# Block-sparse attention with a feed-forward layer on one core: the order of ACT's squares, the type of the sums over partitions, and the step at which a sequence's first queries start

## The chip, the cores and the metric

The kernel runs on one core of one Trainium2 chip. The metric is the device time of one execution in microseconds (us), given as the median of several runs. Lower is better. The core has five engines with a queue each: TensorE (PE; its weight loads are listed apart as PEld), VectorE (DVE), ScalarE (ACT), GpSimd (POOL) and SyncE (SP), which here only issues DMAs.

## The reference

Four sequences of 768 positions go through block-sparse attention with 8 heads of 64, and the result goes through a two-layer feed-forward network with a leaky ReLU:

```python
scores = scale * np.matmul(q, k.transpose(0, 1, 3, 2))
mask = np.abs(blk_i - blk_j) <= window          # blocks of 32, window 1
mask = mask | (blk_i == 0) | (blk_j == 0) | (blk_i == n_blocks - 1) | (blk_j == n_blocks - 1)
...   # and three sampled key blocks for each query block
scores = np.where(mask, scores, -1000000000.0)
attn = np.exp(scores - max); attn = attn / (attn.sum(-1) + 1e-09)
x = (attn @ v)  as (3072, 512)
h = x @ w_in                                    # (512, 2048)
out = np.maximum(0.01 * h, h) @ w_out           # (2048, 512)
```

q, k and v are float32. The two weight matrices arrive as 64-bit floats and are 8 MB each.

## The kernel before

**Number format.** Matmuls take float16. Each operand is split into a high and a low float16 part after it is scaled by a power of two, and the products of the parts are added up in PSUM. The power of two comes from the mean square of the operand: ACT squares the tile and adds up each partition (`square`, line 230), PE adds the 128 partitions with a matmul against a 128x128 tile of ones in float32 (`scale_sum`, line 135), DVE makes the scale from the exponent with four tiny instructions (`scale_of`, lines 149 to 158), ACT writes the high part (line 594 for queries) and DVE the low part (line 596).

**Steps.** The attention is cut into 192 units, one for each pair of heads of each 64 query rows: 48 a sequence, 16 an item (256 query rows). One pass of the main loop is one step: it emits the scores of the next units (`scores`, line 714), a masked copy with the row minimum (`unit_ttr`, line 723), the exponential on ACT (`unit_exp`, line 735), the normalisation, the split in high and low part (lines 762 and 783), the DMA transposes of the split (line 788), attention times values (`pair_av`, line 815), and one chunk of the feed-forward network (`ffn_h` line 850, `ffn_act1`, `ffn_max`, `ffn_act2` lines 856 to 864, `ffn_o` line 877). A string of letters gives the order of these parts within a step. The first unit of a 64-row tile at the head of a sequence has two parts, so the first four units of a sequence have two exponentials each.

**Queries.** A load of queries covers half an item (128 rows, all heads), so there are 24, numbered n, and load n is first used at step 8n. `get_q(n)` issues the DMA (lines 528 to 532, one buffer `rq`); before that it runs the preparation of load n-1 to its end. `start_q(n)` puts the generator `prep_q` in a list, and each step's `side_step` moves every generator on by one stage. The stages of `prep_q` are: the square; nothing; the sum; the scale; the high part; the low part with the DMA transpose `qs_q<-qa_q` (line 599) and the two DMAs `qxs_q<-qs_q` that swap the halves of the partitions (lines 601 and 602). From step 11 on `get_q` is called at steps that leave 3 when divided by 8, and `start_q(n)` at step 8(n-1). Loads 6, 12 and 18 open a new sequence. `start_q(1)` is called at step 0 and again at step 2; the second call replaces the generator, and its key then stands in the list twice.

**Keys, values, weights.** Keys of the next sequence are prepared during the current one in the same manner (`prep_k`, squares at line 230), and so are the values (`prep_v`, written to a scratch tensor in DRAM as hi/lo and gathered from there). The weights are loaded, decoded (lines 363 to 367: one ACT and three DVE instructions a group), summed up in `squares` (line 201, a chain of bfloat16 matmuls) and split (lines 430 and 435) in the first 48 steps. The first two items of the feed-forward network are worked off by quarters of the weights as they come, all others once all weights are ready.

**Order.** A scheduler orders each engine's instructions at compile time by priority and by a simulated timeline: an instruction whose inputs are ready in the simulation can be put ahead of others that were emitted earlier. On the chip each engine then works through its queue in that order. `behind(begin, name)` adds an ordering edge without a semaphore, so that the new instructions stand in the queue after the named one. `square` uses it:

```python
def square(out, in_, ss):
    begin = len(nc.cur_bb.bb.instructions)
    nc.scalar.activation(out, in_, AF.Square, accum_out=ss)
    behind(begin, last_exp[0])
```

`last_exp[0]` is the newest exponential, but before the change it is set from step 48 on only (`CFG["even_at"]` is 48); until then it is `None` and the squares have no such edge.

Of the kernel before, what the change touches and what calls it, by code (L numbers as in the profile page):

```python
# [12 lines left out]
BF16 = mybir.dt.bfloat16  # L13
F32 = mybir.dt.float32
# [5 lines left out]
P = 128  # L20
# [9 lines left out]
CFG = {  # L30
    "ahead": 3,
    "av_lag": 3,
    "bs": 1500,
    "early": 2,
    "even_at": 48,
    "even": 12,
    "flag": 1,
    "g": 2,
# [34 lines left out]
def tile_block_sparse_attention_ffn(  # L73
# [19 lines left out]
    nc = tc.nc  # L93
# [17 lines left out]
    cst = ctx.enter_context(tc.tile_pool(name="cst", bufs=1))  # L111
# [12 lines left out]
    def bank(name, tag="h"):  # L124
        return ps_1.tile([P, 512], F32, tag=tag, name=name, bufs={"h": 3, "av": 1}[tag])
# [1 line left out]

    floor = cst.tile([P, 1], F32, name="floor")
    nc.vector.memset(floor, 1e-9 / PSCALE)
    ones = cst.tile([P, P], F32, name="ones")  # L130
    nc.vector.memset(ones, 1.0)

    def scale_sum(ss, n, name):
        pb = bank(f"{name}_sum")
        nc.tensor.matmul(pb[:, :n], ones, ss, start=True, stop=True)  # L135
        return pb

    def scale_of(pb, n, name, total=False, keep=None, fl="q"):
# [86 lines left out]
    last_exp = [None]  # L225
# [7 lines left out]
    def latest():  # L233
        return nc.cur_bb.bb.instructions[-1].name
# [347 lines left out]
    def prep_q(b, j, i, rq):  # L582

        nm = f"q{b}_{j}_{i}"
        ss = sm.tile([P, 1], F32, tag="ssq", name=f"ss_{nm}")
        qa = pa.tile([P, H, 2, D], F16, tag="qa", name=f"qa_{nm}", bufs=1)
        square(flat(qa)[:, :H * D], rq.rearrange("p h d -> p (h d)"), ss)
        yield 0.7
        yield 0.01
        pb = scale_sum(ss, 1, nm)  # L590
        yield 0.2
        inv, s = scale_of(pb, 1, nm)
        yield 0.4
        nc.scalar.activation(qa[:, :, 1, :], rq, AF.Copy, scale=s[:, :1])
        yield 0.7
        nc.vector.scalar_tensor_tensor(
            out=qa[:, :, 0, :], in0=rq, scalar=s[:, :1], in1=qa[:, :, 1, :], op0=ALU.mult, op1=ALU.subtract)
        qs = pa.tile([P, H, P], F16, tag="qs", name=f"qs_{nm}", bufs=2)
        nc.sync.dma_start_transpose(out=qs, in_=flat(qa))
        qxs = pa.tile([P, H, P], F16, tag="qxs", name=f"qxs_{nm}", bufs=2)  # L600
        nc.sync.dma_start(out=qxs[:D], in_=qs[D:])
        nc.sync.dma_start(out=qxs[D:], in_=qs[:D])
        last_sp["q"] = latest()
        qstack[b, j, i] = (qs, qxs, inv)
        yield 0.8
# [325 lines left out]
    def start(key, gen):  # L931
        gens[key] = gen
        flows.append(key)
# [56 lines left out]
    def refill():  # L990
        for t in list(tasks):
            if t[0] in done and t[1][0].item.nx == TPI:
                hq.extend(t[1])
                tasks.remove(t)
# [32 lines left out]
    def get_q(n):  # L1027
        if n < len(halves):
            if n >= CFG["rq"]:
                until(("q", *halves[n - CFG["rq"]]), lambda: halves[n - CFG["rq"]] in qstack)  # L1030
            rq[n] = load_q(*halves[n])

    def start_q(n):
        if n < len(halves):
            start(("q", *halves[n]), prep_q(*halves[n], rq[n]))

    def get_k(b, hp):
        n = CFG["rk"]
        ob, oh = (b, hp - n) if hp >= n else (b - 1, hp + NP - n)
        if ob >= 0 and b > 0:  # L1040
            until(("k", ob, oh), lambda: (ob, oh) in kready)
        rk[b, hp] = load_k(b, hp)

    def start_k(b, hp):
        start(("k", b, hp), prep_k(b, hp, rk[b, hp]))
# [48 lines left out]
    step = 0  # L1094
# [44 lines left out]
    for u in units:  # L1139
        it, ui = u.item, u.k * NP + u.hp  # L1140
        b, nb = it.b, it.b + 1

        if step == 2:
            start_q(1)
        if step == 6 or step % 8 == 3 and step > 8:
            get_q((step + 5) // 8 + 1)
        if step % 8 == CFG["q_at"] % 8:
            start_q(step // 8 + (2 if CFG["q_at"] < 8 else 1))
        if nb < B:
            g = it.j * 16 + ui  # L1150
            t = g - (CFG["k_at"] if b else CFG["k_at0"])
            every = CFG["k_every"] if b else 5
            if t % every == 0 and 0 <= t // every < NP:
                get_k(nb, t // every)
            if t % every == every - 2 and 0 <= t // every < NP:
                start_k(nb, t // every)
            t = g - CFG["v_at"]
            if t in (0, 2, 4, 6):
                load_v(nb, t // 2)
            if t == 8:  # L1160
                start(("v", nb), prep_v(nb))

        if u.hp == (CFG["g_at"] if step >= 4 else NP - 1) and u.T + 1 < NT:
            start_gather(b, u.T + 1)
        tc.cur_priority = max(tc.cur_priority, 1000 + step * 200)
        if step in ready:
            add_ffn(ready.pop(step))
        refill()
        backlog = len(hq) + sum(len(t[1]) for t in tasks)
        if step < CFG["even_at"]:  # L1170
            credit += max(CFG["rmin"], min(CFG["rmax"], backlog / CFG["spread"]))
            n = int(credit)
            credit -= n
        else:

            n = int(hdone[0] < len(due) and due[hdone[0]] <= step)
        if step == 0:
            scores([u])
        c = aq[0] if aq else None
        for w in CFG["ord1" if step >= CFG["ord1_at"] else "ord"]:  # L1180
            if w == "c" and c:
                ffn_act1(c)
            elif w == "m" and c:
                ffn_max(c)
            elif w == "g" and c:
                ffn_act2(c)
                oq.append(aq.popleft())
            elif w == "S" and step + 1 < len(units):
                ahead = units[step + 1:step + 3]
                if not CFG["spair"]:  # L1190
                    scores(ahead[:1])
                elif u.pi == 1:
                    if any(x.parts > 1 for x in ahead):
                        for x in ahead[:1]:
                            scores([x])
                    else:
                        scores(ahead)
                elif u.parts > 1:
                    scores(ahead[:1])
            elif w == "t":  # L1200
                while live[0] + u.parts > CFG["p"]:
                    if not pend_high and not pend_split:
                        norm_step()
                    high_step()
                    split_step()
                live[0] += u.parts
                unit_ttr(u)
            elif w == "x":
                unit_exp(u)
                if step >= CFG["even_at"]:  # L1210
                    last_exp[0] = latest()
                if u.pi == 1:
                    pend_norm.append(u.pair)
            elif w == "d":
                norm_step()
            elif w == "i":
                high_step()
            elif w == "s":
                split_step()
            elif w == "a":  # L1220
                av_step()
                if vq and vfree[0] and (vq[0][0], "ready") in scr:
                    start_gather_v()
            elif w == "v":
                ev_step()
            elif w == "b":
                do_out()
            elif w == "o":
                do_o(CFG["flag"] if hq or aq else 0)
            elif w == "p":  # L1230
                side_step(CFG["side0"] if step < 16 else CFG["side"])
                gather_step(2)
            elif w == "w":
                wcredit += [r for a, r in CFG["wr"] if step >= a][-1]
                now = tc.cur_priority
                if step < 16:
                    tc.cur_priority = now + CFG["wlate"]
                begin = len(nc.cur_bb.bb.instructions)
                while wcredit >= 1.0:
                    c = next(weights, "end")  # L1240
                    wcredit -= c if c != "end" else wcredit
                if 0 < step < 16:
                    behind(begin, last_ttr[0])
                tc.cur_priority = now
            elif w == "h":
                for i in range(n):
                    if i:
                        do_act()
                        do_o(CFG["flag"])
                    do_h()  # L1250
        step += 1
        if ui == 15:
            ready[step + CFG["lead0" if it.n == 0 else "lead1" if it.n < CFG["early"] else "lead"]] = it
# [62 lines left out]
```

## Time and profile before

| | us |
|---|---|
| median of 3 runs | 842.8 (842.22 to 843.17) |
| profiled execution, device time | 851.52 |
| profiled execution, span of the core | 849.8 |
| PE busy in the span | 749.3 (88%) |
| DVE busy | 595.5 (70%) |
| ACT busy | 507.6 (60%) |
| POOL busy | 352.8 (42%) |

The profiled execution is 8.7 us (1.0%) longer than the median of the runs. Times in the profile count from the start of its span. A row of a timeline has the start, the length, the engine, the line, the operation, out<-in, shapes and count, and in brackets the idle time of the engine ahead of it with what ended it. A row of the chain of work that ended last has the start, the length and what the end was waiting for at that time; a "q" behind an engine's name is its sequencer. A row of a table by stretches has, for each engine, the busy time and the number of instructions, then the granted PE clock as a share of the full one, the share of time in which the DMA engines were busy, and GB/s.

### The profile page before, as it was taken

Reading aid. Unit: us, or ns where it says so; the run is one execution under the profiler, and the core shown is the slowest. Engines: PE = TensorE matmul, PEld = TensorE weight load, DVE = VectorE, ACT = ScalarE, POOL = GpSimd, SP = SyncE. Lnnn points to the kernel's source line nnn. Section 1 sums busy time; section 2 is a strip of 40 time slices with the busy share of each in tenths; the row PEclk is TensorE's granted clock in tenths of the full one; section 3 lists DMA queues with packets and bytes.
Section 4 is the critical chain, followed back from the end, with each engine's and each line's share of the span. In section 5 each row is a group of like instructions: output and inputs, shape, how many; then the busy total and the mean of one; then the engine's idle time right before and its main releaser. Section 6 shows DMA issues by size and latency. Waiting matters only on the chain.

```text
span 849.8 us, 20081 instructions
## 1 busy us (share of the span) xinstructions
PE 749.3 (88%) x7140; PEld 500.6 (59%) x7140; DVE 595.5 (70%) x1595; ACT 507.6 (60%) x1199; POOL 352.8 (42%) x472
## 2 busy tenths in 40 slices
PE   1666675857798999999999999998999999999997
PEld 1455543545465666666666666665666666667664
DVE  5768889898777976867777777678666776651221
ACT  5757678776445766767566667675657556551211
POOL 0218356433233464646343455454244545332221
PEclk9977778989799999999999999999999999999999
DMA  9979289998756999996969999969586766662000
GB/s 198 273 218 247 73 176 240 245 260 147 168 131 106 175 213 190 203 179 146 197 154 154 196 182 186 202 130 204 119 155 150 125 149 139 125 129 35 26 1 25
DMA packets 312004, 135.33 MB, mean 159 GB/s; under 512 B 279774, under 2 KB 292063, under 8 KB 311903
## 3 DMA queue, kind: packets, MB, share of 16 engines
q1 hardware_dynamic: 305262, 113.59, 67.2%
q0 software_dynamic: 6640, 20.45, 9.3%
q8 instruction: 56, 0.92, 0.5%
q14 instruction: 46, 0.37, 0.2%
HBM read 65.58 MB, written 12.58 MB: 92 GB/s over the span
## 4 chain that ended last, share of the span: by engine, by line
PE 70%; DMA 12%; DVE 10%; issue 3%; ACT 2%; SPq 2%; POOL 0%; POOLq 0%; ACTq 0%; DVEq 0%
PE h L850 27%; PE o L877 26%; PE s L714 8%; PE av L815 7%; DMA pt<-pp 3%; DMA wbuf<-in_moe_w_out_dram 2%; DMA qxs_q<-qs_q 2%; DMA qs_q<-qa_q 2%; DVE p L723 2%; DVE pp L783 2%; PE turn L773 2%; DVE W L365 1%; DVE W L435 1%; DVE W L367 1%; PE q_sum L135 1%
## 5 line engine op out<-in xcount | busy, mean ns | idle before, releaser
L877 PE MATMUL o<-W,g 128*128 128x512 f16 x1152 | 270.9, 381 | 6.4 <-DVE ob L898 4.2
L850 PE MATMUL h<-x,W 128*128 128x256 f16 x2304 | 274.2, 277 | 0.2 <-DVE x L833 0.2
L850 PEld LDWEIGHTS <-W 128*128 128x128 f16 x2304 | 225.0, 100 | 37.7 <-issue 3.9
L864 POOL TENSOR_TENSOR g<-ht,g 128x512 f16<-128x512 f32 x96 | 116.9, 1217 | 304.5 <-DVE g L863 254.6
L735 ACT ACTIVATE p<-p,mx 128x384 f32<-128x384 f32 x208 | 126.2, 607 | 158.7 <-DVE mx L723 123.0
L877 PEld LDWEIGHTS <-g 128*128 128x128 f16 x1152 | 108.7, 98 | 125.6 <-issue 10.8
L656 POOL COPY kg<-kt 128x256 f16 x264 | 135.0, 540 | 45.0 <-issue 15.4
L783 DVE SCALAR_TENSOR_TENSOR pp<-p,r,pp 128x384 f16<-128x384 f32 x188 | 120.4, 666 | 24.9 <-ACT pp L762 23.6
L762 ACT ACTIVATE pp<-p,r 128x384 f16<-128x384 f32 x188 | 104.2, 604 | 23.9 <-DVE r L747 10.2
L723 DVE CUSTOM_DVE_ANT_0 p<-s,em,nsc 128x384 f32<-128x384 f32 x176 | 102.0, 608 | 19.8 <-PE s L714 17.1
L683 POOL DMA_INDIRECT vg<-scr,rows x88 | 91.3, 1037 | 50.4 <-issue 20.3
L859 DVE SCALAR_TENSOR_TENSOR ht<-ht 128x512 f32<-128x512 f32 x96 | 67.8, 706 | 53.3 <-ACT ht L856 52.7
L815 PE MATMUL av<-pt,vg 128*64 128x128 f16 x2112 | 82.1, 226 | 10.1 <-DMA pt<-pp 9.6
L815 PEld LDWEIGHTS <-vg 128*64 128x64 f16 x2112 | 73.4, 114 | 27.4 <-issue 21.7
L714 PE MATMUL s<-kg,qs_q 128*64 128x384 f16 x352 | 66.2, 351 | 25.0 <-DVE mx L723 22.7
L856 ACT ACTIVATE ht<-h,gd 128x512 f32<-128x512 f32 x80 | 53.8, 672 | 57.3 <-PE h L850 54.7
L714 PEld LDWEIGHTS <-qs_q 128*64 128x64 f16 x416 | 27.0, 111 | 79.2 <-issue 53.7
L714 PE MATMUL s<-kg,qxs_q 128*64 128x384 f16 x352 | 64.0, 343 | 5.4 <-DMA qxs_q<-qs_q 5.4
L747 DVE RECIPROCAL r<-sum 128x2 f32<-128x2 f32 x96 | 15.4, 161 | 60.2 <-ACT sum L746 57.8
L863 DVE CAST g<-ht 128x512 f16<-128x512 f32 x96 | 41.8, 435 | 9.4 <-PE o L877 7.2
L735 ACT ACTIVATION_READ_ACCUMULATOR p<-p,mx 128x1 f32 x208 | 39.0, 187 | 0.0
L714 PEld LDWEIGHTS <-qxs_q 128*64 128x64 f16 x416 | 26.2, 114 | 20.8 <-DMA qxs_q<-qs_q 9.7
(138 smaller groups left out, 758.0 us busy)
## 6 DMA issues: line engine op xcount, KB each, us to landing
vg<-scr SPq DMA_DIRECT2D x33, 256.0 KB
qxs_q<-qs_q SPq DMA_DIRECT2D x48, 128.0 KB
v<-in_v_dram SPq DMA_DIRECT2D x32, 192.0 KB
scr<-v SPq DMA_DIRECT2D x16, 384.0 KB
W<-in_moe_w_in_dram SPq DMA_DIRECT2D x5, 1024.0 KB
rq<-in_q_dram SPq DMA_DIRECT2D x20, 256.0 KB
out_dram<-ob SPq DMA_DIRECT2D x20, 256.0 KB
rk<-in_k_dram SPq DMA_DIRECT2D x24, 192.0 KB
```

Of the source, the lines that this page charges most:

```text
L656: nc.gpsimd.tensor_copy(out=kg[:, :, slot * BLOCK:(slot + 1) * BLOCK], in_=kt[:, :, bass.ds(off, BLOCK)])
L683: nc.gpsimd.indirect_dma_start(out=vg[:n_, c, :], out_offset=None, in_=scr[b][:, :], in_offset=bass.IndirectOffsetOnAxis(ap=rows[:n_, c - ...
L714: nc.tensor.matmul(o, a, k, start=(n == 0), stop=(n == 1)))
L723: nc.vector.tensor_tensor_reduce(out=u.p[i], in0=u.sp[i], in1=kgs[u.b, u.T][1] if u.T else zero.to_broadcast([P, KEYS]), scale=u.nsc, scal ...
L735: nc.scalar.activation(u.p[i], u.p[i], AF.Exp, scale=-1.0, bias=u.mx[:, :1], accum_out=u.pair.sum[:, u.pi, i:i + 1])
L762: nc.scalar.activation(pp[:, 0, :], p, AF.Copy, scale=u.r)
L783: nc.vector.scalar_tensor_tensor(out=pp[:, 1, :], in0=p, scalar=u.r, in1=pp[:, 0, :], op0=ALU.mult, op1=ALU.subtract)
L815: nc.tensor.matmul(o, a, m, start=(c == 0 and l == 0), stop=(c == n - 1 and l == 1)))
L850: nc.tensor.matmul(c.ph[:, i], w, x, start=(d == 0 and m == 0), stop=(d == NP - 1 and m == 2)))
L859: nc.vector.scalar_tensor_tensor(out=c.t, in0=c.t, scalar=0.01, in1=c.t, op0=ALU.mult, op1=ALU.max)
L864: nc.gpsimd.tensor_tensor(out=c.g[:, 1], in0=c.t, in1=c.g[:, 0], op=ALU.subtract)
L877: nc.tensor.matmul(o, a, w, start=(c.first and i == 0 and m == 0), stop=(c.last and i == 1 and m == 2)))
```

## The change

Three edits:

- `ones` becomes bfloat16, and `scale_sum` reads the upper 16 bits of each float32 partition sum as a bfloat16 (a view, no instruction is added).
- `start_q(12)` is called at step 86 instead of 88 and `start_q(18)` at step 134 instead of 136. These are the first queries of the third and the fourth sequence. All other loads, load 6 too (the test asks for a step of at least 48), keep their step. `get_q` keeps its steps.
- `last_exp[0]` is set after every exponential, so that each square emitted in the main loop before step 48 also stands behind the newest exponential in ACT's queue.

```diff
-    ones = cst.tile([P, P], F32, name="ones")
+    ones = cst.tile([P, P], BF16, name="ones")
     nc.vector.memset(ones, 1.0)
 
     def scale_sum(ss, n, name):
         pb = bank(f"{name}_sum")
-        nc.tensor.matmul(pb[:, :n], ones, ss, start=True, stop=True)
+
+        top = ss.bitcast(BF16).rearrange("p (n l) -> p n l", l=2)[:, :n, 1]
+        nc.tensor.matmul(pb[:, :n], ones, top, start=True, stop=True)
         return pb
...
-        if step % 8 == CFG["q_at"] % 8:
-            start_q(step // 8 + (2 if CFG["q_at"] < 8 else 1))
+
+        n = (step + 2) // 8 + 1
+        if step % 8 == 6 and n % 6 == 0 and step >= CFG["even_at"]:
+            start_q(n)
+        n = step // 8 + 1
+        if step % 8 == 0 and (n % 6 or step < CFG["even_at"]):
+            start_q(n)
...
                 unit_exp(u)
-                if step >= CFG["even_at"]:
-                    last_exp[0] = latest()
+                last_exp[0] = latest()
```

## The prediction

> **What bounds the kernel now.** I read the table by stretches first, because an average over the span mixes two regimes, then the chain of work that ended last, then the idle times in each engine's timeline.
>
> ```profile
> span 849.8 us, 20081 instructions
> 0.00:228.00 228.00, 143.57 (x1370) 99.36 (x1371) 189.74 (x505) 153.31 (x344) 87.32 (x120) 0.86 0.92 206
> 228.00:295.00 67.00, 62.15 (x554) 40.55 (x555) 53.12 (x157) 37.23 (x86) 24.55 (x36) 0.93 0.67 134
> 295.00:770.00 475.00, 469.68 (x4664) 311.68 (x4663) 336.13 (x904) 303.79 (x749) 224.74 (x302) 1.00 0.84 165
> ```
>
> Up to 228 us, while the weights are loaded and decoded, PE is busy 143.57 of 228 us; DVE (189.74) and the DMA engines (0.92) are the full ones there. From 295 to 770 us PE is busy 469.68 of 475 us at a granted clock of 1.00: PE is the bound. So a microsecond taken from PE's stream after about 290 us is a microsecond of the end, and one taken from ACT or DVE there is worth nothing. Before 228 us it is the other way round: what counts is when the weights are ready and PE's stream closes up.
>
> **Sums in bfloat16.** First the sums that lie in the PE-bound stretch, then what one costs on the chain.
>
> ```profile
> L135 PE MATMUL q_sum<-ss_q,ones x32: 250/260/271, 284.8 to 718.0; 128*128 128x1 f32 x32
> L135 PE MATMUL k_sum<-ss_k,ones x16: 167/250/271, 288.5 to 513.8; 128*128 128x1 f32 x16
> L135 PE MATMUL v_sum<-ssv,ones x4: 253/263/273, 389.9 to 562.7; 128*128 128x4 f32 x4
> ...
> 298.75 2.73 PE h L850 x24
> ...
> 427.22 0.31 PE q_sum L135 x2
> 427.53 2.64 PE h L850 x24
> ...
> 153.38 0.91 PE wi_sq L201 x16
> ```
>
> A float32 sum shows as two matmuls, so 32 + 16 + 4 = 52 records from 280 us on are 26 sums. A chunk of `h` takes 2.73 us on the chain without a sum ahead of it, and 0.31 + 2.64 = 2.95 us with one: a sum costs PE 0.22 us. In bfloat16 it is one matmul with a 128x128 weight load; the nearest row is line 201, bfloat16 with 128x128 weights, 0.91 us for 16, so 57 ns each. That saves 0.163 us a sum and 26 x 0.163 = 4.2 us. Bounds: 2.9 us if just one of the two passes goes (26 x 0.11), 5.7 us if the rest is free. The other 26 sums lie before 280 us, where PE has gaps; I count them at 0. The four scale instructions on DVE stay.
>
> [...]
>
> **Queries of a new sequence.** PE's idle times after 295 us are three, and two of them are the scores of a new sequence's first units that wait for `qxs_q<-qs_q`, the last DMA of `prep_q`:
>
> ```profile
> 418.24 0.49 PE L714 MATMUL s<-kt,qxs_q 128*64 128x384 f16 x3 [1.34 <-DMA qxs_q<-qs_q]
> ...
> 592.38 0.82 PE L714 MATMUL s<-kt,qxs_q 128*64 128x384 f16 x3 [2.77 <-DMA qxs_q<-qs_q]
> ...
> 621.57 1.53 PE L815 MATMUL av<-pt,v 128*64 128x128 f16 x48 [1.21 <-DMA pt<-pp]
> ...
> 592.26:595.67 3.41, 3.29 (x34) 2.67 (x35) 1.41 (x5) 1.22 (x5) 0.65 (x1) 0.50 1.03 216
> ```
>
> The second wait costs more than its 2.77 us: for the next 3.41 us the granted clock is 0.50, and half of 3.41, 1.7 us, is lost again. Together 1.34 + 2.77 + 1.7 = 5.8 us. The third wait (1.21 us) is for a transpose of the split behind load 19, which starts at step 144 in both; I leave it in.
>
> [...]
>
> Do two steps do it? Load 12, as it runs now:
>
> ```profile
> 376.01 0.69 SPq L530 DMA_DIRECT2D rq<-in_q_dram  x1
> ...
> 383.23 0.61 ACT L735 ACTIVATE p<-p,mx 128x384 f32<-128x384 f32 x1 [2.15 <-DVE mx L723]
> ...
> 400.48 0.15 DVE L149 TENSOR_SCALAR q_tot<-q_sum 128x1 f32<-128x1 f32 x1
> ...
> 403.43 0.15 DVE L158 RECIPROCAL q_s<-q_inv 128x1 f32<-128x1 f32 x1
> ...
> 408.26 0.74 DVE L596 SCALAR_TENSOR_TENSOR qa_q<-rq,q_s,qa_q 128x512 f16<-128x512 f32 x1
> ...
> 409.03 1.23 SPq L599 DMA_TRANSPOSE qs_q<-qa_q  x1
> ...
> 413.53 0.53 SPq L601 DMA_DIRECT2D qxs_q<-qs_q  x1
> ```
>
> `get_q(13)` at step 91 forces whatever is left of load 12. Started at step 88, that is the scale, the high part, the low part and the DMAs, one behind the other, from 400.48 (the first scale instruction) to 409.03 (the transpose). Started at 86, sum, scale and high part are emitted at steps 88 to 90, and only the low part and the three DMAs are left at step 91, with their input there. The low part can then go as soon as step 91 begins, about where `q_tot` stands now, and DVE has it at some 401 to 404 instead of 408.26. That is 4 to 7 us against a lateness of 1.34 and 2.77 us, so I take the whole 5.8 us; bounds 0 (the next paragraphs) and 5.8. On SP the transpose passes one `pt` transpose and a `scr<-v` store at most; `qs_q` has two buffers, and the older is free. The load is issued at 376.01 and the square would now follow the exponential of step 86 (383.23): 7 us for a load that ACT does not wait for today. Were it late, ACT would wait, but it idles 2.15 us just ahead of that exponential, and PE does not depend on it within the step.
>
> **Squares behind the newest exponential.** Before step 48 the scheduler pulled squares ahead:
>
> ```profile
> ACT qa_q L230 <- DMA rq<-in_q_dram: 12.4, 4, 6.1
> ...
> 54.16 0.63 ACT L230 ACTIVATE qa_q<-rq 128x512 f16<-128x512 f32 x1 [6.13 <-DMA rq<-in_q_dram]
> ...
> 62.70 0.60 ACT L735 ACTIVATE p<-p,mx 128x384 f32<-128x384 f32 x1
> ...
> 82.47 0.63 ACT L230 ACTIVATE qa_q<-rq 128x512 f16<-128x512 f32 x1 [4.55 <-DMA rq<-in_q_dram]
> ...
> 99.25 0.61 ACT L735 ACTIVATE p<-p,mx 128x384 f32<-128x384 f32 x1
> ...
> 55.10 0.17 DVE L747 RECIPROCAL r<-sum 128x2 f32<-128x2 f32 x1 [2.83 <-ACT sum L746]
> ...
> 84.23 0.69 DVE L364 TENSOR_SCALAR W<-W 128x1024 int32<-128x1024 int32 x1 [3.23 <-ACT W L363]
> ...
> 52.86 6.24 DMA qxs_q<-qs_q
> ...
> 74.73 13.71 DMA wbuf<-in_moe_w_out_dram
> ...
> 157.59 0.18 ACT v L230
> ```
>
> The square of load 2, emitted at step 8, stands at 54.16; the exponential of step 8 is at 62.70. ACT blocks 6.13 us on a load that has not landed, and two exponentials, a normalisation (DVE waits 2.83 us for it) and value splits queue behind. The square of load 3 (step 16, exponential at 99.25) blocks ACT for 4.55 us, and a weight decode on DVE waits 3.23 us. With the edge all four waits, 12.4 us of ACT, should go. But both large ones lie beside something longer on the chain: 52.86 to 59.1 is the DMA of load 1, 74.73 to 88.44 the load of a weight group. These end when they end, so most of the 12.4 us is hidden, and the cover is gone only if these DMAs move too. The one square that is itself on the chain is the value square at 157.59 (with its accumulate about 1 us), emitted at step 36 or later, whose exponential comes after 164; behind it, it leaves the chain. I take -1 us for this edit. Bounds: -12.4 (all of it on the path) and, from what becomes late next, the following.
>
> ```profile
> 129.59 0.72 ACT L594 ACTIVATE qa_q<-rq,q_s 128x512 f16<-128x512 f32 x1
> ...
> 135.44 0.60 ACT L735 ACTIVATE p<-p,mx 128x384 f32<-128x384 f32 x1
> ...
> 153.97 0.71 ACT L594 ACTIVATE qa_q<-rq,q_s 128x512 f16<-128x512 f32 x1
> ...
> 164.54 0.60 ACT L735 ACTIVATE p<-p,mx 128x384 f32<-128x384 f32 x1
> ...
> 165.03 1.25 SPq L599 DMA_TRANSPOSE qs_q<-qa_q  x1
> ```
>
> A later square makes a later sum, and then the high part can't be pulled ahead of the step that forces it. Load 4's high part, now at 129.59, would come near the exponential of its forcing step 27 (135.44), 5.8 us later; load 5's, now at 153.97, near that of step 35 (164.54), 10.6 us later. Load 5's transpose is issued at 165.03 today, held by SP's queue, so it loses only what passes that time. Were both delays wholly on the path, with weight loads and `pt` transposes queued behind on SP, they would cost 16.4 us.
>
> **Sum.** 4.2 + 5.8 + 1 = 11.0 us less: 838.8 for the profiled span of 849.8. The profiled execution is 1.0% longer than the median of the runs; I take the same 11.0 us off that median: 842.8 - 11.0 = 831.8.
>
> **Rivals.**
>
> *The queries stay late.* The low part and its DMAs are emitted at step 91 in both versions; if the scheduler keeps DVE's order and the transpose stays near 409, the 5.8 us stay. 842.8 - 4.2 - 1 = 837.6. For it: the forcing step does not move. Against: the scale chain between 400.48 and 408.26.
>
> *ACT's waits were on the path.* All 12.4 us come back instead of 1: 820.4. For it: DVE, the fullest engine up to 228 us, waits 2.83 and 3.23 us just because of these squares. Against: the two DMAs on the chain.
>
> *Queries of the first sequence become late (slower).* Loads 4 and 5 lose 16.4 us in full, and the start of the PE-bound stretch moves with them: 842.8 - 10.0 + 16.4 = 849.2. It decides from 11.7 us of delay on (10.0 of gain and 1.7 to be told). Against: loads 4 and 5 are first used at steps 32 and 40, five steps after the steps that force them.
>
> *No change.* The order of the first 228 us is a product of the simulated timeline; a reshuffle there that costs about the 10.0 us of the other two edits would leave 842.8.
>
> **Numbers.** Forecast (825 to 836): 0.48. Queries stay late (836 to 841): 0.19. ACT's waits on the path (818 to 825): 0.12. No change: 0.09. Slower: 0.12. A change within 0.2% (841.1 to 844.5) can't be told from none. Faster 0.79, same 0.09, slower 0.12. The range 823 to 842 holds the forecast, the late queries, and part of the two cases beside them.
>
> **What would show it.** Sums: one record a sum instead of two, line 135 below 100 ns on the chain. Queries: no idle time for `qxs_q<-qs_q` at line 714 near 410 and 585 us, no half clock there, line 599 of load 12 issued some 4 us earlier against step 91. Squares: no wait of ACT for `rq<-in_q_dram` before 130 us; the last weight decode no later than before. The prediction is wrong if PE's stream closes up later than now (about 290 us) by more than the gain, or if a new idle time takes the place of the two.

## The result, and the profile after

The change made the kernel slower: 854.47 us median (851.70 to 857.77, 5 runs) against 842.80 (841.56 to 843.86, 5 runs), ratio 1.0124 [1.0084, 1.0163]. Compared a second time, the same kernel stood at 1.0169 [1.0120, 1.0218]. The prediction was 831.8. The ratios here and below leave disturbed runs out, the medians do not, so the two can differ by 0.3%.

The profiled execution of after took 857.77 us, 3.3 us above its median; that of before was 8.7 us above its own. So the two spans (856.1 and 849.8) differ by less than the medians do, and I also use a second profile of before (e5, span 840.1).

First the head of the page of after:

```profile
span 856.1 us, 19974 instructions
PE 737.9 (86%) x7088; PEld 487.5 (57%) x7088; DVE 593.4 (69%) x1595; ACT 507.6 (59%) x1199; POOL 346.3 (40%) x472
```

and its table by stretches, cut where the weights end, where PE's stream has closed up, and 475 us on:

```profile
0.00:240.00 240.00, 143.09 (x1407) 96.55 (x1408) 190.00 (x522) 154.13 (x347) 87.69 (x122) 0.82 0.89 200
240.00:300.00 60.00, 56.06 (x497) 37.00 (x495) 48.70 (x142) 34.93 (x82) 23.37 (x35) 0.97 0.66 126
300.00:775.00 475.00, 463.60 (x4627) 304.30 (x4626) 337.35 (x903) 304.88 (x751) 219.07 (x302) 1.00 0.85 165
```

The first stretch holds the work that before did in 228 us (PE 143.09 against 143.57, DVE 190.00 against 189.74) and is 12 us longer; e5 does it in 220 us (PE 141.73, DVE 188.01). In the 475 us of the third row PE is busy 463.60 us, not 469.68 as in the 475 us from 295 us on in before: there is more idle time where PE is the bound (PE's total, 737.9 against 749.3, holds 52 records less, since each sum shows as one and not as two). The sums and the squares' edge themselves did what they should. The groups of line 137 (135 before) from 284 us on:

```profile
L137 PE MATMUL q_sum<-ss_q,ones x16: 167/177/178, 288.7 to 724.3; 128*128 128x1 bf16 x16
L137 PE MATMUL k_sum<-ss_k,ones x8: 163/172/178, 292.2 to 520.8; 128*128 128x1 bf16 x8
L137 PE MATMUL v_sum<-ssv,ones x2: 164/164/164, 397.4 to 570.5; 128*128 128x4 bf16 x2
```

A sum on the chain of work that ended last:

```profile
376.06 0.67 PE av L817 x24
376.73 0.11 PE q_sum L137
376.84 2.64 PE h L852 x24
```

ACT's waits:

```profile
ACT k_k L232 <- DMA kt<-k_k: 11.5, 4, 6.1
ACT qa_q L232 <- DMA rq<-in_q_dram: 0.5, 1, 0.5
```

PE's waits from 300 to 650 us:

```profile
PE av L817 <- DMA pt<-pp: 5.1, 2, 3.3
PE o L879 <- POOL g L866: 2.1, 3, 0.9
PE h L852 <- issue: 1.4, 1, 1.4
PE o L879 <- DVE g L865: 1.2, 1, 1.2
PE s L716 <- DVE mx L725: 0.8, 1, 0.8
PE s L716 <- DMA qxs_q<-qs_q: 0.5, 1, 0.5
```

One record a sum, and 0.11 + 2.64 = 2.75 us for a sum with its chunk, where it was 2.95. ACT waits 0.5 us for queries, where it was 12.4. PE's waits hold 0.5 us for `qxs_q`, where it was 4.1. But they hold 5.1 us for `pt` (1.2 before, 2.5 in e5), 3.3 us for g and 1.4 us of issue ahead of h (nothing of these before). And ACT now waits 11.5 us for `kt<-k_k` (6.0 before). The largest of these waits, from the timelines of ACT, DVE and SP:

```profile
206.46 0.57 ACT L858 ACTIVATE ht<-h 128x512 f32<-128x512 f32 x1
213.12 0.84 ACT L232 ACTIVATE k_k<-rk 128x768 f16<-128x768 f32 x1 [6.08 <-DMA kt<-k_k]
213.96 1.32 ACT L432 ACTIVATE W<-W,wi_s 128x512 f16<-128x512 f32 x2
...
214.70 0.75 DVE L437 SCALAR_TENSOR_TENSOR W<-W,wi_s 128x512 f16<-128x512 f32 x1 [5.54 <-ACT W L432]
...
202.04 7.43 SPq L576 DMA_TRANSPOSE kt<-k_k  x1
228.64 0.35 SPq L358 DMA_DIRECT2D wbuf<-in_moe_w_out_dram  x1
```

A key square of the next sequence stands in ACT's queue ahead of the weights' high parts. Its output buffer is free only when the transpose of the tile before has landed, and ACT blocks 6.08 us on it; DVE's low parts wait 5.54 us behind. In before that square starts at 245.65, behind the weights. The last matmul on the weights moves from 225.66 (218.08 in e5) to 237.85. PE's waits from 100 to 250 us in before, and then in after:

```profile
PE s L714 <- DVE mx L723: 17.4, 8, 4.4
PE av L815 <- DMA pt<-pp: 9.6, 2, 8.5
```

```profile
PE av L817 <- DMA pt<-pp: 31.5, 9, 8.6
PE s L716 <- DMA qxs_q<-qs_q: 9.0, 3, 4.9
PE s L716 <- DVE mx L725: 2.6, 4, 1.0
```

What PE waits for is another thing, and more of it: all rows of these two views together make 50.1 us after and 41.5 before (35.3 in e5). None of the three edits touches a `pt` transpose; the order around it is what is new. Counted in the queues, all five differ from before: the scheduler re-sorted them.

### The profile page after: what moved, and what is told of

The parts are those of the page before. It is cut to its first block, busy times and chain, and to the rows that moved or that the text cites. A ratio compares the mean times of both kernels' runs of the same rounds, so it can differ in the third digit from the quotient of the medians.

```text
span 856.1 us, 19974 instructions
## 1 busy us (share of the span) xinstructions
PE 737.9 (86%) x7088; PEld 487.5 (57%) x7088; DVE 593.4 (69%) x1595; ACT 507.6 (59%) x1199; POOL 346.3 (40%) x472
## 4 chain that ended last, share of the span: by engine, by line
PE 43%; DVE 9%; ACT 7%; DMA 4%; issue 3%; POOL 0%; SPq 0%; ACTq 0%; DVEq 0%; POOLq 0%
PE o L879 18%; PE h L852 17%; PE av L817 4%; PE s L716 4%; DVE pp L785 3%; ACT p L737 2%; DMA pt<-pp 2%; DMA kt<-k_k 2%; DVE p L725 2%; DVE ht L861 1%; ACT pp L764 1%; ACT ht L858 1%; ACT k_k L570 1%; DVE k_k L572 1%; ACT k_k L232 1%
## 5 line engine op out<-in xcount | busy, mean ns | idle before, releaser
L879 PE MATMUL o<-W,g 128*128 128x512 f16 x1152 | 276.2, 384 | 8.1 <-DVE g L865 4.4
L852 PEld LDWEIGHTS <-W 128*128 128x128 f16 x2304 | 221.6, 99 | 41.9 <-issue 6.9
L658 POOL COPY kg<-kt 128x256 f16 x264 | 128.9, 513 | 75.6 <-PE s L716 36.0
L716 PE MATMUL s<-kg,qs_q 128*64 128x384 f16 x352 | 63.1, 347 | 12.0 <-DVE mx L725 7.6
```

The costliest lines, as they stand in the source:

```text
L658: nc.gpsimd.tensor_copy(out=kg[:, :, slot * BLOCK:(slot + 1) * BLOCK], in_=kt[:, :, bass.ds(off, BLOCK)])
L716: nc.tensor.matmul(o, a, k, start=(n == 0), stop=(n == 1)))
L852: nc.tensor.matmul(c.ph[:, i], w, x, start=(d == 0 and m == 0), stop=(d == NP - 1 and m == 2)))
L879: nc.tensor.matmul(o, a, w, start=(c.first and i == 0 and m == 0), stop=(c.last and i == 1 and m == 2)))
```

## Experiments

Every run had the kernel before beside it on its chip (841.97 to 846.02 median there). "Held" means that each engine's queue is fixed in a given order by edges without semaphores:

```diff
+    for packed in kept.values():        # one list of places for each engine
+        ...
+        for one, two in zip(places, places[1:]):
+            tc.add_manual_dep(made[two], made[one].name, mybir.DependencyInfo(
+                mybir.DependencyClass.NoSync, mybir.DependencyReason.DATA), reason="kept")
```

| | kernel | median us | ratio to before |
|---|---|---|---|
| e1 | sums alone, scheduler free | 855.75 | 1.0136 [1.0086, 1.0186] |
| e2 | sums, held in before's order | 843.26 | 0.9986 [0.9950, 1.0022] |
| e3 | squares' edges alone, scheduler free | 853.57 | 1.0093 [1.0055, 1.0132] |
| e4 | queries alone, scheduler free | 843.22 | 1.0021 [0.9988, 1.0055] |
| e6 | float32 sums, held in after's order | 853.12 | 1.0079 [1.0040, 1.0118] |
| e7 | sums and queries, held in e4's order | 843.77 | 0.9996 [0.9951, 1.0040] |
| e8 | before's order, two query squares later | 845.81 | 0.9997 [0.9953, 1.0041] |
| e9 | after's order, the key square later | 850.79 | 1.0078 [1.0041, 1.0114] |
| e10 | after's order to step 48, then e4's | 848.08 | 1.0033 [1.0007, 1.0059] |
| e11 | e4's order to step 48, then after's | 851.00 | 1.0072 [1.0034, 1.0109] |
| e12 | after again | 855.20 | 1.0169 [1.0120, 1.0218] |
| e13 | e10 with the key square later | 848.54 | 1.0067 [1.0039, 1.0096] |
| e14 | queries alone, two steps later | 844.83 | 1.0030 [0.9994, 1.0066] |
| e15 | e13 and two moves on DVE | 846.98 | 1.0005 [0.9970, 1.0040] |
| e16 | e11 with two places mended | 849.22 | 1.0036 [0.9999, 1.0073] |
| e17 | after's order with all these moves | 849.41 | 1.0050 [1.0021, 1.0078] |
| e18 | after's order, held, nothing moved | 852.87 | 1.0085 [1.0057, 1.0112] |

**One edit at a time: e1, e3, e4.**

```diff
 # e1: the first edit only
+    ones = cst.tile([P, P], BF16, name="ones")
 # e3: the third only
-                if step >= CFG["even_at"]:
+                if step >= 0:
 # e4: the second only
+        early = lambda n: n % 6 == 0 and n > 6
+        [start_q(n) for n in range(1, 24) if step == 8 * (n - 1) - (2 if early(n) else 0)]
```

> Only the first edit: the sums over partitions in bfloat16; the scheduler is free to order anew. Theory A (late queries: the squares tied behind the exponentials make the first sequence's queries and with them the weights late, and the other two edits bring what was predicted): 842.8 - 4 = about 839, and the PE stream closes up near 228 us as before. Theory B (reshuffle: the cheaper sums change the simulated timeline, and the new order of all engines' queues costs more than the sums bring): 846 to 856, with the last weight decode several us later than before.

> Only the third edit: squares behind the newest exponential from the first step on. Theory A: 850 to 860, PE waiting for qxs_q in the first 200 us more than before (8.7 us there before). Theory B: 838 to 843, since ACT's waits for the query loads (12.4 us) go.

> Only the second edit: loads 12 and 18 start two steps sooner. Theory A: about 837 (5.8 us less: no idle time for qxs_q near 417 and 590 us, no half clock there). Theory B: 837 to 846, since the order is made anew here too, and the first 300 us stay as before.

The sums alone cost 1.4% and the squares' edges alone 0.9%. Neither adds work, and the losses do not add (1.2 to 1.7% for all three). Both came out where the theory that forecast a loss had them (B for the sums, A for the edges). Each changes the order of the queues; for the edges this does not tell their own effect, squares held back and queries late behind them, from the re-sorting around it (PE waits 19.3 us for `qxs_q` in the first 250 us of e3, 8.7 in before). The query edit leaves the queues as they were until about step 86, and it is the one that costs nothing; it does not bring theory A's 5.8 us in the median either. In e1 the dense stretch has waits that before does not have (300 to 650 us):

```profile
PE av L815 <- DMA pt<-pp: 5.6, 3, 2.3
PE k_sum L135 <- ACT k_k L230: 3.7, 2, 2.8
PE s L714 <- DMA qxs_q<-qs_q: 3.7, 2, 1.9
PE h L850 <- ACT ht L856: 1.0, 1, 1.0
```

**The edit without the order, the order without the edit: e2, e6, e7.** Each holds the queue order of another kernel, as in the diff above, and differs from that kernel in the sums alone: e2 has before's order with sums in bfloat16, e6 after's order (its queries and edges too) with float32 sums, e7 e4's order with sums in bfloat16.

> The sums in bfloat16, but every engine's queue held in exactly the order that it had before, by ordering edges without semaphores. Theories A and B both: 835 to 840 (the predicted 4.2 us for the 26 sums in the PE-bound stretch, perhaps some more from the 26 earlier ones). If it is not faster than before, the sums' price itself was wrong.

> The changed kernel's order of every engine's queue, held by ordering edges, with the float32 sums of before. Theory B (order): 853 to 859, as slow as the changed kernel or up to 4 us slower, although not one instruction differs from the kernel before but in its place. If the bfloat16 sums themselves cost something, it comes out near 843.

> Edits one and two without the reshuffle of the first: bfloat16 sums, loads 12 and 18 two steps sooner, every queue held in the order that the second edit alone gives. Theory B: 835 to 841, the fastest so far. If the sums in an unchanged order bring nothing (ratio 0.9986 before) and the queries neither (1.0021), 843.

With before's order the sums cost nothing (e2, against 1.0136 with the scheduler free). With after's order and float32 sums (e6) the kernel is slow. So the order makes the loss, not what the instructions do. It is far from a local change: to turn e7's order into after's, with the same instructions, at least 632 of PE's 7026 instructions and 296 of DVE's 1379 have to move. e7 has two of the three edits at before's time; the third adds no instruction, only the order. But the gains that were expected of e2 (835 to 840) and e7 (835 to 841) do not show in their medians; the stretch behind step 48, further down, shows something of them.

e5 is the kernel before once more, to see how far its profile moves: 841.79 us, and step 48 comes at 241.6 us where the first profile has 250.7.

> The kernel before, unchanged, for a second profile. The first profile (851.52 us) is 8.7 us above the median of its runs. Theory C: that profile is no typical execution, and the two waits for qxs_q near 417 and 590 us with their half clock are smaller or absent in a typical one, so that two steps sooner had less than 5.8 us to win. Against it: the waits are there in the traces of the kernels with the same queries (1.34 and 2.77; 2.98 and 1.63; 1.71 and 2.57 us), and the first 300 us are what differs.

**Do ACT's waits for queries matter? e8.** Before's order is held, but the squares of loads 2 and 3 stand 3 and 6 places later on ACT:

```diff
 # ACT's queue
-    qa_q<-rq (squares of loads 2 and 3)     in before's places
+    qa_q<-rq (squares of loads 2 and 3)     behind one exponential each
```

> The kernel before in its own order, but the squares of loads 2 and 3 stand three and six places later in ACT's queue, behind one exponential each, so that ACT no longer waits 6.1 and 4.6 us for their loads. Cover theory (the prediction's: these waits lie beside longer DMAs): 841 to 844. Path theory (the waits were on the path): 832 to 838.

Ratio 0.9997. ACT's waits for `rq` are 4.7 us there (12.4 and 5.8 in the two profiles of before):

```profile
ACT qa_q L230 <- DMA rq<-in_q_dram: 4.7, 3, 3.5
```

The 832 to 838 us of the path theory did not come. That the waits are hidden is not shown by it, though: the square of load 2 still waits 3.55 us in e8, and beside the second profile of before just 1.1 us of such waits is gone. The two profiles of before differ by 6.6 us in these waits and by 9.1 us at step 48, and two profiles do not tell which follows from which.

**Where in the span: e10, e11.** The queues switch from one order to the other behind the exponential of step 48.

```diff
-    kept = after's order                 # or e4's
+    kept = after's order up to the exponential of step 48, e4's behind it    # e10
+    kept = e4's order up to the exponential of step 48, after's behind it    # e11
```

> The first two edits (bfloat16 sums, queries sooner), with every engine's queue in the order of the changed kernel up to the exponential of step 48 (some 250 us) and behind it in the order of the kernel that has the query edit alone. That order kept throughout gave 843.77; the changed kernel's throughout, with single-precision sums, 853.12. If the loss is made in the part with the weights and the first two sequences' loads (theory E: 8.5 us there between the two profiles, 255.7 against 247.2 at step 48): 850 to 853, ratio 1.007 to 1.011. If it is made in the dense stretch behind it (theory D: step 48 to 64 and 64 to 191 were 3.3 and 4.2 us slower in the profile): 846 to 849, ratio 1.002 to 1.006.

> The converse: every queue in the order of the kernel with the query edit alone up to the exponential of step 48, and behind it in the order of the changed kernel. Theory E (loss made before step 48): 844 to 846, ratio 1.000 to 1.003. Theory D (loss made behind it): 849 to 852, ratio 1.006 to 1.010. If the two halves add, the excess of this run and of the run with the orders the other way round make together the 10 us between the two whole orders; if they do not, the orders do not fit together at the seam.

The two halves cost 0.33% and 0.72%, 2.1 and 5.0 us in the medians: the loss lies on both sides of step 48. Both ratios are in theory D's ranges, but theory D has no loss ahead of step 48, and e10's interval excludes 1. The sum, 7 us, is about what e6 and e18 lose (8.9 and 8.5). Which half is larger stays open, since the intervals overlap. In the profiles step 48 comes at 250.3 to 255.7 us where the order up to it is after's (after, e6, e10, e12, e18) and at 240.1 to 250.7 where it is before's (before, e2, e4, e5, e7, e8, e11, e14), and the stretch from there to step 191 takes 508.7 us in e11, 507.1 in e10 and 503.4 in e7, which has the order of e10 there. e11 shows what the later part consists of (PE's waits from 300 to 640 us, then the timeline of ACT and PE):

```profile
PE av L815 <- DMA pt<-pp: 4.8, 2, 3.1
PE o L877 <- POOL g L864: 2.1, 3, 0.9
PE k_sum L135 <- ACT k_k L230: 1.8, 1, 1.8
PE h L850 <- ACT ht L856: 1.0, 1, 1.0
```

```profile
509.61 0.84 ACT L230 ACTIVATE k_k<-rk 128x768 f16<-128x768 f32 x1 [5.35 <-DMA kt<-k_k]
...
510.60 0.16 PE L135 MATMUL k_sum<-ss_k,ones 128*128 128x1 bf16 x1 [1.83 <-ACT k_k L230]
511.77 0.57 PE L850 MATMUL h<-x,W 128*128 128x256 f16 x2 [1.01 <-ACT ht L856]
```

Again a key square holds ACT (5.35 us) for a transpose. This time PE pays at once: the sum waits for the square, and `h` waits for `ht`, which stands behind the square on ACT.

**Which places: e9, e13, e15, e16, e17, with e12 and e18 for comparison.** In e9 and e13 one instruction moves:

```diff
 # ACT's queue, e9 in after's order, e13 in e10's
-    k_k<-rk (third key square)     ahead of the weights' last high parts
+    k_k<-rk (third key square)     behind the weights' last decode (line 363)
```

> The queues of the changed kernel on every engine, with one instruction moved: ACT's third key square of the second sequence (k_k<-rk, which stood 6.08 us on ACT at 207 to 213 us for a transpose, ahead of the weights' high parts) now stands behind the last decode of the weights (232.72 in that profile), still ahead of its sum on PE at 241.38. Theory A, that this wait delays the weights and these the steps behind them: ACT's 6.08 us at 207 are gone, the last matmul of the weights comes at 230 to 233 us instead of 238.0, step 48 comes some 5 us sooner, 847 to 850 us, ratio 1.004 to 1.009. Theory B, that the weights' late end is covered or bound by something else (decode, the transfers): the last matmul stays within 2 us of 238 or step 48 does not move, 852 to 855, ratio 1.009 to 1.015.

> The order of the changed kernel up to the exponential of step 48, with ACT's third key square of the second sequence behind the weights' last decode, and behind step 48 the order of the kernel with the query edit alone. The same without the moved square gave ratio 1.0033. Theory A (that square's 6.08 us wait is the early loss): 1.000 within 0.3%, 842 to 846 where the kernel before is 844, and step 48 some 3 to 5 us after step 46 sooner than in the run without (50 us from step 46 to 48 where that had 52.9). Theory B (the early loss is spread over many waits): again 1.002 to 1.005, and the 52.9 us stay within 1 us.

The wait is gone from ACT in both. In e9 the last matmul on the weights comes at 231.03 us, and the ratio, 1.0078, lies in theory A's range; but e18, the same order with nothing moved, stands at 1.0085, so no gain is shown. In e13 step 48 comes 52.4 us after step 46, within 1 us of the 52.9 without the move, as theory B expected, and the ratio did not fall (1.0067 beside 1.0033). Theory A, that this one wait is the early loss, is not borne out. The trace of e13 shows why a removed wait need not help. On DVE:

```profile
215.69 0.76 DVE L364 TENSOR_SCALAR W<-W 128x512 int32<-128x512 int32 x2
216.36 0.42 DVE L833 TENSOR_TENSOR x<-xf,x 128x256 f16<-128x256 f32 x1
220.09 0.75 DVE L898 SCALAR_TENSOR_TENSOR ob<-o,beta,ob 128x512 f32<-128x512 f32 x1 [3.31 <-PE o L877]
220.76 0.68 DVE L859 SCALAR_TENSOR_TENSOR ht<-ht 128x512 f32<-128x512 f32 x1
221.36 0.68 DVE L365 SCALAR_TENSOR_TENSOR W<-wbuf,W 128x512 int32<-128x512 int32 x1
```

DVE reaches the weights' decode sooner, and then waits 3.31 us for PE's output, which stands ahead of the rest of the decode (line 365). So e15, e16 and e17 mend the next places too:

```diff
 # e15, DVE: lines 365, 364, 365 and the cast g (863) go ahead of ob (898)
 # e16, 316 us: ACT's ht (856) and DVE's 859, 863 go ahead of the exponentials and pp
 # e16, 509 us: ACT's k_k<-rk goes behind the exponential and ht
 # e17: after's order with e9's, e15's and e16's moves
```

> The kernel with the moved square and the query edit's order behind step 48 (ratio 1.0067), with two more moves on DVE: three instructions of the weights' decode (lines 365, 364, 365, 1.8 us) go ahead of the output addition ob (line 898) for which DVE idled 3.31 us at 217 us, and the cast g (line 863), for which PE's o waited 2.88 us, goes ahead of the second ob. Theory G (the early loss sits in what stands in front of the weights on one engine after the other): the last weight load on SP comes 2 to 4 us sooner against step 46, PE's 2.88 us wait falls below 1, and the ratio is 1.001 to 1.004. Theory H (spread over many places; each removed wait is replaced by the next): the last matmul of the weights moves by less than 1.5 us against step 46, ratio 1.005 to 1.008.

> The kernel with the query edit's order up to step 48 and the changed kernel's behind it (ratio 1.0072), with two places of the dense stretch mended: at 316 us ACT's ht (line 856) and DVE's two instructions for g (lines 859 and 863) go ahead of the exponentials and of pp (PE's o waited 0.46 and 0.93 us there); at 509 us ACT's key square, which stood 5.35 us for the transpose kt<-k_k, goes behind the exponential and ht (PE waited 1.83 us for k_sum and 1.01 us for ht). Theory G: these waits of PE, 4.2 us, shrink to 1 to 2, and the ratio falls to 1.003 to 1.005. Theory H: they go, others come, ratio 1.006 to 1.009.

> The whole order of the changed kernel with all these moves: the key square behind the weights, the decode and g ahead of ob, and the two places of the dense stretch. The changed kernel stood at 1.0124 and 1.0169. Theory G: 1.003 to 1.008. Theory H: 1.010 to 1.015.

> The changed kernel itself, beside the next two on one chip. Both theories: ratio 1.008 to 1.016, as before (1.0124, and 1.0079 with its order and single-precision sums).

> The first two edits with every engine's queue held in the order of the changed kernel, nothing moved: the same program as the changed kernel. If the loss is the order's and its halves add (2.1 and 5.0 us in the medians), ratio 1.007 to 1.011, and the moved square is worth 0 to 3 us. If the two halves make more together than apart, 1.012 to 1.017, and the moved square is worth 5 us or more.

With all moves after's order stands at 1.0050 [1.0021, 1.0078], against 1.0124, 1.0169 and 1.0085 with none: some 40 to 70% of the loss is gone with nine instructions moved. That is within what theory G expected, and the interval lies apart from those of the first two runs of after, though it overlaps that of e18, the closest comparison. e16 (1.0036) lies within G's range as well and e15 (1.0005) below it, but their intervals touch those of e13 and e11, and the traces speak for theory H. In e15 the weights do not end sooner against step 46 (36.5 us behind it, 35.9 in e13). In e16 PE's waits from 300 to 640 us make 12.3 us, 10.9 in e11, and from step 48 to 191 it takes 512.9 us, not less than e11's 508.7. PE's waits in e15 between 195 and 260 us are others than in e13, not fewer:

```profile
PE av L815 <- DMA pt<-pp: 5.9, 2, 5.7
PE wo_sq L201 <- DVE W L367: 2.5, 2, 1.6
PE o L877 <- DVE g L863: 1.9, 1, 1.9
```

So what each single place is worth stays open; together they carry perhaps half, and beside e18 even that is not clear of the noise.

**Queries two steps later: e14.**

```diff
-        [start_q(n) ... if step == 8 * (n - 1) - (2 if early(n) else 0)]
+        [start_q(n) ... if step == 8 * (n - 1) - (-2 if early(n) else 0)]
```

> The kernel before with the query edit alone turned round: the queries of the third and fourth sequence are begun two steps later than before (steps 90 and 138 in place of 88 and 136), not two sooner; the queues are the kernel before's up to step 90. Theory C, that late queries cost what the prediction worked out for them (5.8 us for two steps): PE's waits for qxs and the half clock behind them grow by some 4 to 8 us behind step 90, 848 to 852, ratio 1.005 to 1.010. Theory F, that the time before the queries is slack that is made up later, or that their stalls are filled by other work: ratio 0.997 to 1.003.

PE's waits from 290 us on in e14, and then in e4:

```profile
PE s L714 <- DMA qxs_q<-qs_q: 3.2, 2, 1.9
PE av L815 <- DMA pt<-pp: 0.8, 1, 0.8
```

```profile
PE av L815 <- DMA pt<-pp: 0.8, 2, 0.6
```

Two steps sooner the wait for `qxs_q` is gone; two steps later it is no longer than in before (4.1 and 3.3 us in its two profiles). Theory C expected 4 to 8 us more of these waits and is out by the trace; the interval of the ratio, 1.0030 [0.9994, 1.0066], covers most of theory F's range and reaches into the lower end of theory C's.

## Why the prediction was wrong

**The step that failed is the sum itself.** "The sum" added what each edit does to instructions whose order was taken as given, apart from the moved squares. The prediction had the other case as a rival, *No change*: a reshuffle that costs "about the 10.0 us of the other two edits", confined to the first 228 us, at a chance of 0.09. So the sum had no term for the new order. The runs showed one: after's order alone, with float32 sums, is 8.9 us slower than before in the medians (e6), and the whole change 11.7 us, where 11.0 us less was forecast. A loss came from two of the edits, each alone; it lies on both sides of step 48; and it is more than the edits bring. A sum that takes 0.2 us less of PE, or an edge on a square, changes the simulated timeline, and the scheduler answers in all five queues.

**Sums in bfloat16: right in kind, a little small.** 0.20 us a sum on the chain (2.95 to 2.75), not 0.163, so 26 x 0.20 = 5.2 us, between the 4.2 and the bound of 5.7. The sum now lengthens the chunk by 0.02 us (2.75 against 2.73), though its own row, 0.11 us, is just above the 100 ns that I had named as a sign. In e2, with before's order, the stretch from step 48 to 191 is 4.6 to 5.2 us shorter than in the two profiles of before. The weight load of a sum was no measure of its price: the 26 loads of `ones` from 284 us on in after take 95 to 98 ns each, but run beside other matmuls (the one at 376.66 us, for example, beside `av`, which ends on the chain at 376.73), and the chain grows by the 0.02 us above. The exponentials of steps 48 and 191 start, by the timelines:

| | step 48 | step 191 | between |
|---|---|---|---|
| before | 250.7 | 760.4 | 509.7 |
| e5 (before again) | 241.6 | 750.7 | 509.1 |
| e2 (sums, held) | 248.0 | 752.5 | 504.5 |
| e4 (queries) | 248.4 | 753.3 | 504.9 |
| e7 (both) | 247.2 | 750.6 | 503.4 |
| after | 255.7 | 766.6 | 510.9 |
| e12 (after again) | 251.9 | 762.5 | 510.7 |
| e18 (after, held) | 255.6 | 767.1 | 511.5 |

**Queries: the mechanism right, the size near the measured one.** In e4 both waits and the half clock are gone (the rows of load 18's first scores, 584.91 to 586.06 us, take 0.33 to 0.35 us each there, and 0.53 to 0.82 us at the half clock in before). Load 12's transpose was issued at 392.67 instead of 409.03, its low part at 391.90 instead of 408.26, sooner than the 401 to 404 that I worked out:

```profile
391.90 0.74 DVE L596 SCALAR_TENSOR_TENSOR qa_q<-rq,q_s,qa_q 128x512 f16<-128x512 f32 x1
...
392.67 1.23 SPq L599 DMA_TRANSPOSE qs_q<-qa_q  x1
```

From step 48 to 191 e4 is 4.2 to 4.8 us shorter than before; I had 5.8, of which 1.7 was a half clock that the second profile of before does not have (a granted clock of 1.00 from 300 to 640 us in e5). But the median of e4 does not show it (1.0021 [0.9988, 1.0055]); the first 48 steps move by some 9 us between two profiles of the same kernel (241.6 and 250.7), and a gain of 0.5% is at the edge of what 12 runs resolve. In e7 the gains do not add: 503.4, some 6 us less than before where 5.2 and 4.5 would make 9.7. What is late next is the third wait that I left in. I had it at 1.21 us (it is 2.12 in e5); e7 has:

```profile
611.18 2.13 PE L815 MATMUL av<-pt,v 128*64 128x128 f16 x36 [3.90 <-DMA pt<-pp]
```

It grew by 1.8 to 2.7 us, and the granted clock is 0.88 in the mean from 607.2 to 622 us in e7, about what 3.41 us at half clock (1.7 us lost) make. It is 2.9 to 4.4 us in the kernels e9, e10, e11, e13 and e15 to e18 as well, 2.54 in e2, and 0.6 in e4.

**Squares: what becomes late was seen, and left out of the sum.** ACT's waits for `rq` are gone but for 0.5 us. That most of the 12.4 us was hidden fits e8, but e8 does not show it. I looked for what becomes late among the queries of loads 4 and 5, and that came. Load 4's high part runs 12.5 us later (129.59 before), where I had 5.8, and load 5's 7.8 us later, where I had 10.6. PE's waits for `qxs_q` in the first 250 us are, before and after (6.3 us in e5):

```profile
PE s L714 <- DMA qxs_q<-qs_q: 8.7, 3, 3.2
```

```profile
PE s L716 <- DMA qxs_q<-qs_q: 21.2, 6, 6.3
...
142.13 0.71 ACT L596 ACTIVATE qa_q<-rq,q_s 128x512 f16<-128x512 f32 x1
```

What these waits cost is open, since they stand in part in the place of waits for `mx` (21.9 us before, 5.6 after). What I did not look for is a key square that became early. "Behind the newest exponential" holds a square back, and does not keep it from blocking ACT further on. But e9 and e13, which move it, show no gain, so it is not shown to be the larger cost.

**The rival that forecast slower** (849.2) had the sign and one part of the mechanism, the late queries of the first sequence; but e1, which has no such edge, loses as much. The chance of 0.12 for slower was too low for two edits that change the scheduler's input, and no row of a profile of before can show the order that it will find.

**What stays open.** Which places of the new order carry the loss, and how much of it the late queries are; why e13 and e9 did not gain by the wait that they lost; and whether the sums and the queries, in a held order, gain the 4 to 6 us that the traces show from step 48 on, or less (e2, e4 and e7 lie between -0.5% and +0.6%). No kernel run here is shown to beat the kernel before.

## What to carry to other kernels

Where a scheduler orders the queues at compile time, an edit has two costs: its own, and that of the order that comes out. Compare the queues of both kernels first, and hold the old order to measure the edit, or the new order without the edit to measure the order; these two runs (e2 and e6) settled the cause here. In after an instruction that waited for a buffer held up its queue (`k_k`, with ACT idle for 6.08 us and the weights' high parts behind it): look for squares and copies of the next piece of work that stand ahead of this one's. But do not price such a wait at its length: that one was moved away and no gain was seen; in the trace of e13 DVE then waited for the next thing.

## What the runs showed of the hardware

The half clock did not go by the length of the idle time ahead of it alone. In after PE idled 2.01 us up to 275.87 us and 3.28 us up to 627.05 us; behind each the granted clock was 0.50 for 3.41 us (275.9 to 279.3 and 627.5 to 630.9). In before a spell of 3.41 us followed 2.77 us of idle time (592.3 to 595.7), and another 1.16 us (278.2 to 281.7), while 1.80 us up to 267.81 and 1.34 us up to 418.24 were followed by a clock of 1.00. The records change the clock at points that lie whole multiples of 3.41 us apart (in before at 216.8, 227.0, 233.9, 278.2 and 281.7 us, which is 3, 2, 13 and 1 times 3.41 us from one to the next; the clock is 1.00, 0.50, 1.00 and 0.50 between them). What decides is not shown: no run varied where an idle time falls between these points.

The same program's first 250 us, in which the DMA engines are busy 0.89 of the time (before, 0 to 250 us), differ by some 9 us between two profiles, while the stretch from step 48 to 191 differs by 0.6 us (509.7 and 509.1). So does the changed kernel: 255.7 and 251.9 us at step 48 in after and e12, and 510.9 and 510.7 us from there to step 191. In these pairs the spread comes from the first stretch; what in it varies is not shown.
